# Two pairs' values in one burst at a fused kernel's entry, and an order corrected by a table

## The chip, the cores and the metric

The kernel runs on one core of a Trainium2 chip. Its five engines run side by side and each works through its own instructions in a fixed order: PE (TensorE, matrix products; its weight loads are shown as PEld), DVE (VectorE), ACT (ScalarE), POOL (GpSimd) and SP, which here only issues transfers. The metric is the device time of one execution in microseconds; smaller is better.

## What is computed

Block-causal attention (4 batches, 8 heads, 576 tokens, 64 channels) and two feed-forward layers behind it, all in float32:

```
scores = scale * q @ k.T ; masked where block(i) < block(j), blocks of 64 tokens
attn = exp(scores - rowmax) ; attn = attn / (rowsum + 1e-9)
x = attn @ v                              -> 2304 tokens x 512
x = max(x @ w1, x @ w2, x @ w3) @ w_out   -> 768 wide inside
out = relu(x @ w_in)**2 @ w_out2          -> 2048 wide inside
```

## The kernel before, in words

**Pairs and groups.** Two heads of one batch make a pair; there are 16 pairs, four per batch. The 576 query rows of a pair are cut into two groups: group 0 (rows 0 to 255, steps 0 and 1) and group 1 (rows 256 to 575, steps 2 and 3 and a last half step). A step multiplies scores (tile `sc`), takes the row maximum on DVE (`nm`), the exponential and its row sum on ACT (`P`, `sm`), transposes `P` on PE (`tp`) and copies the result to SBUF: `ta` for group 0, `tb` and `t4` for group 1. Then `values` multiplies the transposed probabilities with v (tile `av`).

**Direct pairs.** For the four pairs of batch 0 the probabilities are not normalised. `sum_rows` spreads the reciprocal row sums over the channels with small products (tile `r`), and DVE multiplies `av` with them. The products `av` and `r` use weights of 64 columns ("narrow"), the two heads side by side; all others load 128 columns ("wide"). A run of narrow products between wide ones is called a burst here.

**The entry.** All four pairs do group 0 first, then group 1. In the same time the weights of the first layer (18 chunks `w1`, 6 chunks `wo1`) are loaded as raw 64-bit words, and each is turned into a high and a low float by two ACT instructions, two DVE instructions, one POOL addition, an ACT copy (high part) and a DVE subtraction (low part). The token block 0 (256 tokens, group 0 of batch 0) goes through the first layer (`l`, from `xhl`, the split of x) between the steps of group 1. The other blocks and batches follow, then the second layer, a stream of products with 384 columns (`ph`, `acc`).

**What sets the order.** The code only records operations. `Plan.issue` then places them: it keeps a modelled clock per engine, and at each step gives the engine that is free first the ready operation of the lowest rank, ties broken by the order of recording. Every instruction is therefore recorded at one helper line of the profile. The plan is made while the program is built; on the chip each engine follows its list and waits where data is missing. The first call of `issue` covers everything up to token block 3; a second call covers the rest.

Of the kernel before, what the change touches and what calls it, by code (L numbers as in the profile page):

```python
# [12 lines left out]
F32 = mybir.dt.float32  # L13
# [10 lines left out]
B, H, S, D = 4, 8, 576, 64  # L24
NPAIR = H // 2
# [12 lines left out]
TAIL = 512  # L38

GROUPS = ((0, 256), (256, 320))  # L40
GA, GB = 256, 320
# [106 lines left out]
        return View(t, t.area)  # L148


class Op:
    def __init__(self, index, engines, name, args, kw, rank):
        self.index, self.engines, self.name, self.args, self.kw, self.rank = index, engines, name, args, kw, rank
        self.deps, self.after, self.makes = set(), [], []
        self.engine = self.end = None

# [15 lines left out]
class Plan:  # L172
# [53 lines left out]
            (v.tile.writes if any(v is x for x in out) else v.tile.reads).append((op, v.area))  # L226
        return op

    def issue(self):

        ops, free, held, queue = self.ops, self.free, self.held, self.queue
        left = [0 for op in ops]
        users = [[] for _ in ops]
        for op in ops:
            for d in (*op.deps, *op.after):
                if d.end is None:
                    left[op.index] += 1
                    users[d.index].append(op)
        waiting = {e: {} for e in free}
        narrow = False  # L240

        def offer(op):
            for e in op.engines:
                when = 0.0
                for d in op.deps:
                    when = max(when, d.end + ((SEM[d.engine] + (500 if e == 'pe' else 100 if e == 'pool' else 0)) if d.engine != e else 0))
                waiting[e][op.index] = when, shares_port(e, op)

        for op in ops:
            if not left[op.index]:  # L250
                offer(op)
        for _ in ops:
            best = None
            for e, w in waiting.items():
                if not w:
                    continue
                other = held["pool" if e == "dve" else "dve"] if e in held else 0.0
                start = {i: max(free[e], at, other if port else 0.0) for i, (at, port) in w.items()}
                t = min(start.values())
                i = min((i for i, s in start.items() if s <= t), key=lambda i: (ops[i].rank, i))  # L260
                if best is None or t < best[0]:
                    best = t, e, i
            t, e, i = best
            op = ops[i]
            op.engine = e
            length = duration(e, op) * SLOW[e]
            if e == "pe":
                length += SWITCH * (columns(op) != narrow)
                narrow = columns(op)
            if e in held and waiting[e][i][1]:  # L270
                held[e] = t + length - HOLD[e]
            for other in op.engines:
                del waiting[other][i]
            if e == "sp":
                queue = max(t + 1700, queue) + transfer(op)
                op.end, free[e] = queue + 300, t + 465
            else:
                op.end = t + length
                free[e] = op.end - LAP[e]
            for tile in op.makes:  # L280
                tile.make()
            self.tc.keep_in_program_order(self.call(self.real[e], alias(e, op.name), op.args, op.kw))
            for u in users[i]:
                left[u.index] -= 1
                if not left[u.index]:
                    offer(u)
        self.ops, self.queue = [], queue
# [74 lines left out]
def fused_kernel(ctx: ExitStack, tc: tile.TileContext, z0, k0, kz0, qk, v, w123, wo1, win2, wo2, out):  # L362
# [164 lines left out]

    ops, x_t = {}, {}
    turn, late = [0], []
    marks = []  # L530

    def new_xf(n):
# [19 lines left out]
    def attn_pair(n, groups=(0, 1)):  # L552
# [5 lines left out]
        direct = n < NPAIR  # L558


        if 0 in groups:
            ta = at.tile([128, 2, GA + 128], F32, tag="ta", bufs=CFG["TB"][0], name=f"ta{n}")
        if 1 in groups:
            tb = [at.tile([128, 4, GB], F32, tag="tb", bufs=2 * CFG["TB"][1], name=f"tb{n}_{h}") for h in range(2)]
            t4 = at.tile([128, 2, 64], F32, tag="t4", bufs=2, name=f"t4_{n}")
        xf = None if direct else new_xf(n)

# [7 lines left out]
        def reciprocals(sm):  # L575
            nc.vector.tensor_scalar(out=sm, in0=sm, scalar1=1e-9, scalar2=None, op0=ALU.add)
            nc.vector.reciprocal(out=sm, in_=sm)


        def step(i):  # L580
            N = 128 * (i + 1)
            name = f"{n}_{i}"

            share = i < 2
            sc = [bank(f"sc{name}_{h}", sc_tag(i)) for h in range(1 if share else 2)]
            P = [at.tile([128, 576], F32, tag="P", bufs=PB, name=f"P{name}_{h}") for h in range(len(sc))]
            if share:
                both = sc[0][:, :2 * N].rearrange("p (h k) -> p h k", h=2)
                sc = [both[:, h] for h in range(2)]
                P = [P[0][:, N * h:N * h + N] for h in range(2)]  # L590
            nm = small(f"nm{name}")
            scale = SCALE if sf else 1.0
            sm = sums[i // 2][:, 2 * (i % 2):2 * (i % 2) + 2] if direct else small(f"sm{name}")
            for h in range(2):
                for c, (qp, kp) in enumerate(score[h]):
                    mm(sc[h][:, :N], qp[:, 128 * i - q0:128 * i - q0 + 128], kp[:, :N], start=c == 0,
                       stop=c == len(score[h]) - 1)
                if not share:
                    nc.vector.memset(sc[h][0:64, N - 64:N], MASKED / scale)
                    nc.vector.tensor_reduce(out=nm[:, h:h + 1], in_=sc[h][:, :N], axis=AX.X, op=ALU.max, negate=True)  # L600
            if share:
                nc.vector.memset(both[0:64, :, N - 64:N], MASKED / scale)
                nc.vector.tensor_reduce(out=nm, in_=both, axis=AX.X, op=ALU.max, negate=True)
            if sf:
                nc.vector.tensor_scalar(out=nm, in0=nm, scalar1=SCALE, scalar2=None, op0=ALU.mult)
            for h in range(2):
                act = nc.scalar.activation(out=P[h][:, :N], in_=sc[h][:, :N], func=AF.Exp, bias=nm[:, h:h + 1],
                                           scale=scale, accum_out=sm[:, h:h + 1])
            if not direct:
                reciprocals(sm)  # L610
                for h in range(2):
                    nc.vector.tensor_scalar(out=P[h][:, :N], in0=P[h][:, :N], scalar1=sm[:, h:h + 1], scalar2=None,
                                            op0=ALU.mult)
            marks.append((act,))
            to = 128 * i - (0 if share else GA)
            tp = [bank(f"tp{name}_{h}", "tp") for h in range(1 if share else 2)]
            for h in range(2):
                t, o = (tp[0], N * h) if share else (tp[h], 0)
                for j in range(i + 1):
                    nc.tensor.transpose(t[:, o + 128 * j:o + 128 * j + 128], P[h][:, 128 * j:128 * j + 128], ident)  # L620
                if not share:
                    cp(CFG["EV2"][h], out=tb[h][:, :i + 1, to:to + 128], in_=t[:, :N].rearrange("p (j q) -> p j q", q=128))
            if share:
                cp(CFG["EV"][i], out=ta[:, :, to:to + N], in_=tp[0][:, :2 * N].rearrange("p (h k) -> p h k", h=2))


        def last_step():
# [17 lines left out]
            marks.append((act,))  # L645
            tp, tq = bank(f"tp{n}_t", "tp"), bank(f"tq{n}_t", "tp")
            for j in range(4):
                nc.tensor.transpose(tp[:, 128 * j:128 * j + 128], P[:, 128 * j:128 * j + 128], ident)
            nc.tensor.transpose(tq[:, :128], P[:, S - 128:], ident)
            for h in range(2):  # L650
                cp("a", out=tb[h][:, :, TAIL - GA:], in_=tp.rearrange("p (j h q) -> p h j q", h=2, j=4)[:, h])
            cp("a", out=t4, in_=tq[:, :128].rearrange("p (h q) -> p h q", h=2))


        def values(g):
            a, w = GROUPS[g]
            acc = bank(f"av{n}_{g}", "av" if g or direct else "tp")
            if g == 0:
                mv = [(0, 0, [ta[:, h, :GA] for h in range(2)]), (1, 128, [ta[:, h, GA:] for h in range(2)])]
            else:  # L660
                mv = [(j, 0, [t[:, j] for t in tb]) for j in range(3)]
                mv += [(3, 128, [t[:, 3, 128:] for t in tb]), (4, 256, [t4[:, h] for h in range(2)])]
            for c, (j, o, p) in enumerate(mv):
                for h in range(2):
                    mm(acc[64 * h:64 * h + 64, o:w], vals[h][j], p[h], start=c == 0, stop=c == len(mv) - 1)
# [12 lines left out]

        def sum_rows(g):
            sm = sums[g]  # L680
            reciprocals(sm[:, :4 + g])
            rows = bank(f"r{n}_{g}", "tp")
            for i in range(2 + g):
                for h in range(2):
                    c, o, m = (2 * i + h, 0, 128) if i < 2 else (4, 64 * h, 64)
# [4 lines left out]
        if 0 in groups:  # L690
# [1 line left out]
                step(i)  # L692
                yield
            if direct:
                values(0)
        if 1 in groups:
            for i in range(2, 4):
                step(i)
                yield
            last_step()  # L700
            yield
            if not direct:
                values(0)
            values(1)

    def split_x(b, j):
        with nc.ranked(CFG["PX"]):
# [149 lines left out]
    with nc.behind(marks[CFG["WO"]][0]), nc.ranked(2):  # L857
        for q in range(NQ):
            quad_forms(1, q)
        for q in range(EARLY):  # L860
            quad_forms(0, q)
    nc.issue()
    es_a.close()


# [310 lines left out]
```

## Time and profile before

| | us |
|---|---|
| median of 3 runs (lowest, highest) | 840.61 (840.38, 841.45) |
| the profiled execution | 840.18 |
| its span, first to last instruction | 838.4 |

The table compares like with like only within a line: the span leaves out what lies around the program, 1.78 us in the profiled execution. That execution is 0.43 us faster than the median. In the rows below "busy" of PE counts a product from its start to its modelled end, and products overlap, so that PE's real pace is read from starts, one product to the next.

### The profile page before, as it was taken

The page shows a single profiled execution, that of the slowest core. Times are in us where ns is not written, and L with a number is a line of the kernel's source. Part 1 is how long each engine was busy: PE and PEld are TensorE (multiplying, and loading weights), DVE is VectorE, ACT ScalarE, POOL GpSimd, SP SyncE. Part 2 cuts the span into 40 slices and gives each one's busy share as a digit, 9 for nine tenths or more (in the row PEclk, how much of TensorE's full clock was granted, in tenths as well). Part 3 has the DMA queues.
Part 4 walks back from the last instruction along what each step waited for, and adds up shares of the span by engine and source line. Part 5 has one row for each costly group of instructions (what it writes and reads, how often), then busy time and mean ns, then how long its engine had stood idle before and what let it go on. Part 6 is the DMA issues. An engine that isn't in the chain of part 4 may idle for free.

```text
span 838.4 us, 14621 instructions
## 1 busy us (share of the span) xinstructions
PE 825.8 (99%) x5008; PEld 779.2 (93%) x5008; DVE 625.0 (75%) x1347; ACT 474.4 (57%) x1099; POOL 108.0 (13%) x98
## 2 busy tenths in 40 slices
PE   8999999999999999999999999999999999999998
PEld 6678899988999889999999999999999999999998
DVE  7989789888889988817877557987269855478562
ACT  7999678788778767736554224544124552233441
POOL 2343111221122212202221000000000000000000
PEclk9999999999999999999999999999999999999999
DMA  9755455665566656254796867888988889988882
GB/s 326 263 162 171 124 175 182 203 224 183 167 206 206 199 192 201 77 194 150 264 352 228 312 203 248 286 292 271 306 257 255 257 249 288 293 256 254 246 272 85
DMA packets 92203, 190.24 MB, mean 227 GB/s; under 512 B 9697, under 2 KB 18913, under 8 KB 92129
## 3 DMA queue, kind: packets, MB, share of 16 engines
q1 hardware_dynamic: 92128, 189.31, 69.2%
q8 instruction: 40, 0.66, 0.3%
q14 instruction: 35, 0.28, 0.1%
HBM read 150.47 MB, written 38.80 MB: 226 GB/s over the span
## 4 chain that ended last, share of the span: by engine, by line
PE 90%; DVE 5%; ACT 3%; DMA 1%; POOL 1%; issue 1%; POOLq 0%; ACTq 0%; DVEq 0%
PE l L190 33%; PE ph_x L190 12%; PE acc_x L190 12%; PE ph_z L190 9%; PE acc_z L190 6%; PE av L190 4%; PE sc L190 4%; PE tp L190 3%; PE acc_y L190 3%; PE sc_t L190 2%; DVE nm L190 1%; DMA raw_w<-in_wo 1%; PE tp_t L190 1%; DVE w1l L190 1%; ACT P L190 1%
## 5 line engine op out<-in xcount | busy, mean ns | idle before, releaser
L190 PE MATMUL l<-xhl,w1h 128*128 128x432 f32 (+2 forms) x864 | 230.6, 344 | 0.5 <-DVE xhl L190 0.5
L190 PEld LDWEIGHTS l<-xhl,w1h 128*128 128x128 f32 x864 | 154.0, 188 | 7.5 <-DVE xhl L190 1.2
L190 PE MATMUL l<-xhl,w1l 128*128 128x432 f32 (+2 forms) x432 | 149.7, 347 | 0.6 <-DVE run L190 0.5
L190 PEld LDWEIGHTS l<-xhl,w1l 128*128 128x128 f32 x432 | 81.3, 188 | 5.8 <-DVE run L190 1.4
L190 PE MATMUL ph_x<-t,ws 128*128 128x384 f32 x432 | 80.9, 335 | 0.0
L190 PE MATMUL l<-hh,wo 128*128 128x432 f32 (+2 forms) x288 | 77.5, 344 | 1.2 <-DVE wo L190 1.1
L190 PEld LDWEIGHTS ph_x<-t,ws 128*128 128x128 f32 x432 | 75.6, 188 | 0.0
L190 ACT ACTIVATE P<-sc,nm 128x128 f32<-128x128 f32 (+3 forms) x128 | 67.3, 535 | 11.5 <-DVE nm L190 10.0
L190 DVE TENSOR_TENSOR run<-l,run 128x432 f32<-128x432 f32 (+2 forms) x72 | 39.8, 553 | 32.6 <-PE l L190 29.4
L190 POOL TENSOR_TENSOR f_w<-f_w,raw_w 128x512 int32<-128x512 int32 x30 | 41.5, 1384 | 148.2 <-DVE f_w L190 33.4
L190 DVE TENSOR_REDUCE nm<-sc 128x2 f32<-128x256 f32 (+2 forms) x96 | 55.0, 590 | 0.8
L190 PEld LDWEIGHTS l<-hh,wo 128*128 128x128 f32 x288 | 51.9, 188 | 3.7 <-DVE wo L190 1.3
L190 PE MATMUL acc_x<-g_p,ws 128*128 128x384 f32 x288 | 54.0, 335 | 0.0
L190 PE MATMUL ph_z<-b,ws 128*128 128x384 f32 x288 | 53.9, 335 | 0.0
L190 PE MATMUL tp<-ident,P 128*128 128x128 f32 x320 | 49.9, 275 | 1.1 <-ACT rs L190 0.5
L190 PEld LDWEIGHTS acc_x<-g_p,ws 128*128 128x128 f32 x288 | 50.5, 188 | 0.0
L190 PEld LDWEIGHTS ph_z<-b,ws 128*128 128x128 f32 x288 | 50.4, 188 | 0.0
L190 PE MATMUL l<-hl,wo 128*128 128x432 f32 (+2 forms) x144 | 49.2, 342 | 0.0
L190 PEld LDWEIGHTS tp<-ident,P 128*128 128x128 f32 x320 | 38.8, 141 | 8.9 <-ACT P L190 1.3
L190 PE MATMUL av<-tb,v 128*64 128x320 f32 (+1 forms) x256 | 42.9, 410 | 0.0
L190 ACT COPY tb<-tp 128x384 f32<-128x384 f32 (+1 forms) x64 | 32.4, 539 | 13.4 <-PE tp L190 12.9
L190 DVE TENSOR_TENSOR g_p<-c_wo,g_p 128x768 fp32r<-128x768 f32 x24 | 22.9, 956 | 16.8 <-ACT g_p L190 16.8
(188 smaller groups left out, 1746.5 us busy)
## 6 DMA issues: line engine op xcount, KB each, us to landing
ws<-ws_d SPq DMA_DIRECT2D x336, 256.0 KB, 4.0
ws_d<-wst SPq DMA_DIRECT2D x70, 256.0 KB, 4.4
raw<-in_qk SPq DMA_DIRECT2D x24, 576.0 KB, 4.3
ws_d<-wst SPq DMA_DIRECT2D x21, 512.0 KB, 7.1
raw_w<-in_w SPq DMA_DIRECT2D x18, 512.0 KB, 4.8
raw_w<-in_wo SPq DMA_DIRECT2D x16, 512.0 KB, 4.3
raw_wi<-in_win SPq DMA_DIRECT2D x14, 512.0 KB, 5.8
v<-in_v SPq DMA_DIRECT2D x16, 320.0 KB, 3.8
```

Source lines behind the costliest of these rows:

```text
L190: return getattr(engine, op_name)(*map(value, args), **{k: value(x) for k, x in kw.items()})
```

## The change

**One burst for two pairs.** In batch 0 an even pair's `values` is kept back and called together with the odd pair's, behind the last copy of the odd pair's transposed probabilities (`done`). So `av` and `r` of two pairs stand in one burst, for either group. For this the odd pair's probabilities go into `home`, a tile in the place of a later x buffer (`xf`), which is empty at that time; `region` finds a chunk's place in it, and the transposes of four chunks are written in a rotated order so that the chunks fit there. The two pairs' `av` of group 0 share one PSUM bank, half each; the odd pair's `av` of group 1 takes a bank of the tag `tp`, its row sums one of the tag `sc`.

**The table.** `issue` gets a list `MOVES` of 424 entries (index of an operation, addition to its rank, addition to its place among equals). It changes the order of the first `issue` all through, on all engines.

```
+MOVES = (
+    (8, -17, -1159), (14, -28, -1568), (16, -16.5, 1598), (17, -11.5, 85), (18, -8.5, 1150), (19, -28.5, -2404),
...
+    def issue(self, moves=()):
...
+        for i, rank, place in moves:
+            ops[i].place = ops[i].rank + rank, ops[i].index + place
...
+                i = min((i for i, s in start.items() if s <= t), key=lambda i: ops[i].place)
...
+    def second():
+        if "home" not in held:
+            held["home"] = m1.tile([128, NPAIR, S], F32, tag="xf", bufs=2, name="home").rearrange("p k s -> p (k s)")
+        return held["home"]
...
+        odd = direct and n % 2
         if 0 in groups:
-            ta = at.tile([128, 2, GA + 128], F32, tag="ta", bufs=CFG["TB"][0], name=f"ta{n}")
+            if odd:
+                ta = second()[:, :2 * (GA + 128)].rearrange("p (h k) -> p h k", h=2)
+            else:
+                ta = at.tile([128, 2, GA + 128], F32, tag="ta", bufs=CFG["TB"][0], name=f"ta{n}")
...
+        def both_values(g):
+
+            reciprocals(sums[g][:, :4 + g])
+            if not odd:
+                held[g] = values
+                return
+            with nc.behind(done[0]):
+                held.pop(g)(g)
+                values(g)
...
+            if direct and g == 0:
+                if not odd:
+                    held["acc"] = bank(f"av{n}_{g}", "av")
+                acc = held["acc"][:, GA * (n % 2):GA * (n % 2) + GA]
+            else:
+                acc = bank(f"av{n}_{g}", "av" if g and not odd else "tp")
...
-            reciprocals(sm[:, :4 + g])
-            rows = bank(f"r{n}_{g}", "tp")
+            rows = bank(f"r{n}_{g}", "sc" if odd and g else "tp")
...
             if direct:
-                values(0)
+                both_values(0)
...
-            if not direct:
+            if direct:
+                both_values(1)
+            else:
                 values(0)
-            values(1)
+                values(1)
...
-    nc.issue()
+    nc.issue(MOVES)
```

The order on PE in the entry. The first number behind a tile's letters is the pair, so `av1_0` is group 0 of pair 1. Before, the burst of pair 1 stands alone between wide products:

```order
L190 MATMUL sc3_0_0_251<-zk_early_107 128x128
L190 MATMUL sc3_1_0_258<-zk_early_107 128x256
L190 MATMUL sc0_2_0_275<-k0_143,z0_qs_139 128x384
L190 MATMUL av1_0_280<-ta1_240,v1_0_103 64x256 x2
L190 MATMUL av1_0_280<-ta1_240,v1_0_103 64x128 x2
L190 MATMUL r1_0_292<-ident_60,sm1_0_203 64x128 x4
L190 MATMUL tp2_0_0_304<-ident_60,P2_0_0_272 128x128 x2
```

Now pairs 0 and 1 stand in one burst (pair 1 writes the other half of the tile `av0_0`):

```order
L269 MATMUL sc3_0_0_240<-zk_early_105 128x128
L269 MATMUL av0_0_243<-ta0_180,v0_0_80 64x256 x2
L269 MATMUL av0_0_243<-ta0_180,v0_0_80 64x128 x2
L269 MATMUL r0_0_255<-ident_60,sm0_0_153 64x128 x4
L269 MATMUL av0_0_243<-home_228,v1_0_110 64x256 x2
L269 MATMUL av0_0_243<-home_228,v1_0_110 64x128 x2
L269 MATMUL r1_0_274<-ident_60,sm1_0_208 64x128 x4
L269 MATMUL sc3_0_0_240<-zk_early_105 128x128
```

The narrow work of two pairs has become one run, later in pair 0's case and with one way in and one way out.

At the end of batch 0, PE's rows around the row sums of pair 3 before, a burst of their own inside the second product of the first layer (`l2`):

```order
L190 MATMUL sc4_2_0_1305<-kh_4_0_1270,qs_4_0_1225 128x384
L190 MATMUL l2_0_1_1255<-hl0_743,wo1_1057 128x256
L190 MATMUL r3_1_1308<-ident_60,sm3_1_1064 64x128 x4
L190 MATMUL r3_1_1308<-ident_60,sm3_1_1064 64x64 x2
L190 MATMUL l2_0_1_1255<-hh0_680,wo1_1057 128x256
```

Now, behind the products of `l2` on the weight chunks 0 to 3, the burst of pairs 2 and 3 begins (32 narrow products, of which these are the first):

```order
L269 MATMUL l2_0_1_1212<-hl0_753,wo1_1045 128x256
L269 MATMUL l2_0_1_1212<-hh0_739,wo1_1045 128x256
L269 MATMUL r3_1_1249<-ident_60,sm3_1_1087 64x128 x3
L269 MATMUL r3_1_1249<-ident_60,sm3_1_1087 64x64
L269 MATMUL av2_1_1254<-tb2_0_865,v2_1_749 64x320
L269 MATMUL av2_1_1254<-tb2_1_935,v2_1_749 64x320
L269 MATMUL r2_1_1259<-ident_60,sm2_1_835 64x128 x3
L269 MATMUL r2_1_1259<-ident_60,sm2_1_835 64x64 x2
L269 MATMUL av3_1_1270<-home_228,v3_1_789 64x320 x3
```

Three runs (pair 2's burst, `av3_1`, `r3_1`), which lay apart before, have become one, and it stands between the uses of chunk 3 and chunks 4 and 5 of `wo1`.

On DVE the low part of chunk 3 of `wo1` (the subtraction `wo1<-f_wo1_3`) stood behind the split of the next x block (`xhl1`) before:

```order
L190 TENSOR_TENSOR run0_5_2_1233<-l1_0_5_2_1206,run0_5_1_1208 128x256
L190 CAST xhl1_1238<-xf0_647 128x320
L190 CAST hh0_680<-run0_5_2_1233 128x256
L190 TENSOR_TENSOR xhl1_1238<-xf0_647,xhl1_1238 128x320
L190 TENSOR_TENSOR hl0_743<-run0_5_2_1233,hh0_680 128x256
L190 TENSOR_TENSOR xhl1_1238<-xf0_647,xhl1_1238 128x320 x2
L190 TENSOR_TENSOR wo1_1057<-f_wo1_3_1124,wo1_1057 128x512
```

Now it stands before it:

```order
L269 TENSOR_TENSOR run0_5_1_1177<-l1_0_5_1_1124,run0_5_0_1100 128x256
L269 TENSOR_SCALAR f_wo1_4_1154<-f_wo1_4_1154 128x512
L269 TENSOR_TENSOR run0_5_2_1182<-l1_0_5_2_1148,run0_5_1_1177 128x256
L269 TENSOR_TENSOR wo1_1045<-f_wo1_3_1112,wo1_1045 128x512
L269 TENSOR_SCALAR nm3_t_1126<-nm3_t_1126 128x1
L269 TENSOR_TENSOR hl0_753<-run0_5_2_1182,hh0_739 128x256
```

The subtraction has moved ahead of the x splits: 192 DVE instructions stand ahead of it instead of 202.

## Rows read from the trace of the kernel before

**Rows 1.** The page's busy times: busy us (share of the span), instructions.

```profile
PE 825.8 (99%) x5008; PEld 779.2 (93%) x5008; DVE 625.0 (75%) x1347; ACT 474.4 (57%) x1099; POOL 108.0 (13%) x98
```

**Rows 2.** Busy us by stretch: stretch, length, PE, PEld, DVE, ACT, POOL; clock; DMA.

```profile
10.00:32.00 22.00, 19.54 (x137) 12.61 (x136) 21.86 (x64) 20.45 (x62) 7.60 (x6) 1.00 0.90 315
32.00:85.00 53.00, 51.91 (x388) 42.12 (x387) 47.83 (x119) 50.37 (x124) 22.04 (x16) 1.00 0.57 182
97.00:360.00 263.00, 261.64 (x1700) 240.05 (x1700) 228.41 (x652) 201.31 (x563) 54.51 (x54) 1.00 0.57 183
440.00:838.40 398.40, 394.80 (x2245) 392.67 (x2243) 261.22 (x382) 147.38 (x241) 2.82 (x2) 1.00 0.80 256
```

**Rows 3.** Timeline of PE, one whole burst: start us, us, product, records.

```profile
40.69 0.28 PE L190 MATMUL l<-xhl,w1l 128*128 128x256 f32 x1
40.81 0.40 PE L190 MATMUL l<-xhl,w1h 128*128 128x256 f32 x2
41.14 2.16 PE L190 MATMUL av<-tb,v 128*64 128x320 f32 x16
...
43.24 0.72 PE L190 MATMUL r<-ident,sm 128*64 128x128 f32 x12
43.90 0.38 PE L190 MATMUL l<-xhl,w1l 128*128 128x256 f32 x1
44.12 0.40 PE L190 MATMUL l<-xhl,w1h 128*128 128x256 f32 x2
```

**Rows 4.** Timeline of PE: pair 3's two bursts and the wait behind them.

```profile
89.13 2.16 PE L190 MATMUL av<-tb,v 128*64 128x320 f32 x16
...
91.34 0.39 PE L190 MATMUL l<-hh,wo 128*128 128x256 f32 x1
91.56 0.28 PE L190 MATMUL l<-hl,wo 128*128 128x256 f32 x1
...
92.90 0.77 PE L190 MATMUL r<-ident,sm 128*64 128x128 f32 x12
93.60 0.38 PE L190 MATMUL l<-hh,wo 128*128 128x256 f32 x1
93.82 0.56 PE L190 MATMUL sc<-kl,qs 128*128 128x128 f32 x3
...
96.24 0.39 PE L190 MATMUL l<-hh,wo 128*128 128x256 f32 x1 [1.13 <-DVE wo L190]
```

**Rows 5.** Timeline of DVE: low parts of wo1's chunks 3 and 4, and 5.

```profile
89.32 1.29 DVE L190 TENSOR_TENSOR wo<-f_wo,wo 128x512 fp32r<-128x512 f32 x2
...
95.49 0.69 DVE L190 TENSOR_TENSOR wo<-f_wo,wo 128x512 fp32r<-128x512 f32 x1 [0.17 <-ACT wo L190]
```

**Rows 6.** Waits of DVE from 10 to 97: us in total, times, longest us.

```profile
DVE sc L190 <- PE sc L190: 2.5, 4, 1.2
DVE nm_t L190 <- PE sc_t L190: 1.5, 2, 0.8
DVE sm L190 <- ACT P_t L190: 0.9, 1, 0.9
```

**Rows 7.** Waits of PE over the span, same columns.

```profile
PE sc L190 <- DMA zk<-in_k: 1.4, 1, 1.4
...
PE tp_t L190 <- DVE P_t L190: 0.6, 1, 0.6
...
PE tp L190 <- ACT rs L190: 0.5, 1, 0.5
...
PE sc_t L190 <- ACT P L190: 0.5, 1, 0.5
...
PE sc L190 <- ACT P L190: 0.2, 1, 0.2
```

**Rows 8.** Instructions by tile, `w1l`: ns min/median/max, first and last start.

```profile
L190 DVE TENSOR_TENSOR w1l<-f_w,w1h x12: 669/684/1720, 17.6 to 71.1; 128x512 fp32r<-128x512 f32 x12
```

**Rows 9.** Timeline of POOL and DVE around the longest of these.

```profile
22.09 1.30 POOL L190 TENSOR_TENSOR f_w<-f_w,raw_w 128x512 int32<-128x512 int32 x1 [1.82 <-ACT raw_w L190]
22.21 1.72 DVE L190 TENSOR_TENSOR w1l<-f_w,w1h 128x512 fp32r<-128x512 f32 x1
```

More of the change, by code (lines that the diff above doesn't have):

```diff
@@ L148, in tile @@
         return View(t, t.area)
+MOVES = (
[74 rows of a table added]
+)
 class Op:
@@ L153, in __init__ @@
         self.index, self.engines, self.name, self.args, self.kw, self.rank = index, engines, name, args, kw, rank
+        self.place = rank, index
         self.deps, self.after, self.makes = set(), [], []
@@ L227, in note @@
         return op
-    def issue(self):
+    def issue(self, moves=()):
         ops, free, held, queue = self.ops, self.free, self.held, self.queue
+        for i, rank, place in moves:
+            ops[i].place = ops[i].rank + rank, ops[i].index + place
         left = [0 for op in ops]
@@ L259, in issue @@
                 t = min(start.values())
-                i = min((i for i, s in start.items() if s <= t), key=lambda i: (ops[i].rank, i))
+                i = min((i for i, s in start.items() if s <= t), key=lambda i: ops[i].place)
                 if best is None or t < best[0]:
@@ L529, in fused_kernel, with region @@
     turn, late = [0], []
+    held = {}
+    def second():
+        if "home" not in held:
+            held["home"] = m1.tile([128, NPAIR, S], F32, tag="xf", bufs=2, name="home").rearrange("p k s -> p (k s)")
+        return held["home"]
+    def region(t, base, first, chunks, a, e):
+        start, w = base + GB * first + a, e - a
+        o = min(start, t.area.shape[1] - GB * chunks)
+        return t[:, o:o + GB * chunks].rearrange("p (j q) -> p j q", q=GB)[:, :, start - o:start - o + w]
     marks = []
@@ L558, in attn_pair @@
         direct = n < NPAIR
+        odd = direct and n % 2
         if 0 in groups:
-            ta = at.tile([128, 2, GA + 128], F32, tag="ta", bufs=CFG["TB"][0], name=f"ta{n}")
+            if odd:
+                ta = second()[:, :2 * (GA + 128)].rearrange("p (h k) -> p h k", h=2)
+            else:
+                ta = at.tile([128, 2, GA + 128], F32, tag="ta", bufs=CFG["TB"][0], name=f"ta{n}")
         if 1 in groups:
-            tb = [at.tile([128, 4, GB], F32, tag="tb", bufs=2 * CFG["TB"][1], name=f"tb{n}_{h}") for h in range(2)]
+            if odd:
+                tb = [(second(), (4 * GB - 128) * h - 128) for h in range(2)]
+            else:
+                tb = [(at.tile([128, 4, GB], F32, tag="tb", bufs=2 * CFG["TB"][1],
+                               name=f"tb{n}_{h}").rearrange("p j q -> p (j q)"), 0) for h in range(2)]
             t4 = at.tile([128, 2, 64], F32, tag="t4", bufs=2, name=f"t4_{n}")
@@ L577, in reciprocals @@
             nc.vector.reciprocal(out=sm, in_=sm)
+        done = []
+        def both_values(g):
[6 more added lines that the diff above has]
+                values(g)
         def step(i):
@@ L619, in step @@
                 for j in range(i + 1):
-                    nc.tensor.transpose(t[:, o + 128 * j:o + 128 * j + 128], P[h][:, 128 * j:128 * j + 128], ident)
+                    to_j = o + 128 * ((j + 1) % 4 if i == 3 else j)
+                    nc.tensor.transpose(t[:, to_j:to_j + 128], P[h][:, 128 * j:128 * j + 128], ident)
                 if not share:
-                    cp(CFG["EV2"][h], out=tb[h][:, :i + 1, to:to + 128], in_=t[:, :N].rearrange("p (j q) -> p j q", q=128))
+                    cp(CFG["EV2"][h], out=region(*tb[h], i == 2, i + 1, to, to + 128),
+                       in_=t[:, :N].rearrange("p (j q) -> p j q", q=128))
             if share:
-                cp(CFG["EV"][i], out=ta[:, :, to:to + N], in_=tp[0][:, :2 * N].rearrange("p (h k) -> p h k", h=2))
+                done[:] = [cp(CFG["EV"][i], out=ta[:, :, to:to + N], in_=tp[0][:, :2 * N].rearrange("p (h k) -> p h k", h=2))]
         def last_step():
@@ L647, in last_step @@
             for j in range(4):
-                nc.tensor.transpose(tp[:, 128 * j:128 * j + 128], P[:, 128 * j:128 * j + 128], ident)
+                o = 128 * ((j + 1) % 4)
+                nc.tensor.transpose(tp[:, o:o + 128], P[:, 128 * j:128 * j + 128], ident)
             nc.tensor.transpose(tq[:, :128], P[:, S - 128:], ident)
             for h in range(2):
-                cp("a", out=tb[h][:, :, TAIL - GA:], in_=tp.rearrange("p (j h q) -> p h j q", h=2, j=4)[:, h])
-            cp("a", out=t4, in_=tq[:, :128].rearrange("p (h q) -> p h q", h=2))
+                cp("a", out=region(*tb[h], 0, 4, TAIL - GA, GB), in_=tp.rearrange("p (j h q) -> p h j q", h=2, j=4)[:, h])
+            done[:] = [cp("a", out=t4, in_=tq[:, :128].rearrange("p (h q) -> p h q", h=2))]
         def values(g):
             a, w = GROUPS[g]
-            acc = bank(f"av{n}_{g}", "av" if g or direct else "tp")
+            if direct and g == 0:
[4 more added lines that the diff above has]
+                acc = bank(f"av{n}_{g}", "av" if g and not odd else "tp")
             if g == 0:
@@ L660, in values @@
             else:
-                mv = [(j, 0, [t[:, j] for t in tb]) for j in range(3)]
-                mv += [(3, 128, [t[:, 3, 128:] for t in tb]), (4, 256, [t4[:, h] for h in range(2)])]
+                mv = [(j, 0, [region(*t, j + 1, 1, 0, GB)[:, 0] for t in tb]) for j in range(3)]
+                mv += [(3, 128, [region(*t, 0, 1, 128, GB)[:, 0] for t in tb]), (4, 256, [t4[:, h] for h in range(2)])]
             for c, (j, o, p) in enumerate(mv):
@@ L701, in attn_pair @@
             yield
-            if not direct:
+            if direct:
+                both_values(1)
+            else:
                 values(0)
-            values(1)
+                values(1)
     def split_x(b, j):
```

73 rows, old and new, of the table MOVES are left out of this document.

## The prediction, made before the changed kernel was run

> **What bounds the kernel now.** I read the page first, then the busy times by stretch, then PE's timeline and the waits of PE and DVE, and last the timelines around the places where PE stands still.
>
> On the page PE looks full [rows 1]: 825.8 of 838.4 us. The stretches say where that is true [rows 2]. From 440 us on PE is busy for 394.8 of 398.4 us and nothing else comes near; the change leaves the order there as it is but for a few rows at the seam, so I put that part at no change. From 97 to 360 PE is busy for 261.6 of 263 us, with DVE at 87%. But from 10 to 32 us DVE is busy for 21.86 of 22 us, so that it has no free time at all, and from 32 to 85 us ACT is busy for 50.37 of 53 us and DVE for 47.83. There three engines run side by side, each nearly full. What they race for shows at 96.24 us: PE has waited 1.13 us for DVE's last weight conversion [rows 4]. From that product on PE runs through with few waits. So the kernel's time is the moment at which PE passes this product (the first use of chunk 5 of `wo1`), plus the PE work behind it, plus the later waits. I make the sum in these three terms.
>
> The same stretches also speak against the change: in the entry it lightens PE, while ACT and DVE, whose work stays the same, are as full [rows 2]. The Trainium skill (Perfetto Trace Analysis, Identifying the Most-Contended Engine) calls the engine with the highest occupancy the one to improve, and wants TensorE judged by its weight loads; by these, PE is at 42.12 of 53 us in that stretch and ACT and DVE come first, so PE's savings there would be worth nothing. That is the second rival below, worked out from rows.
>
> **Seven bursts fewer.** The order has 23 bursts of narrow products before and 16 now: in batch 0, six of group 0 become two and five of group 1 become two; the twelve of the later batches stay. The price of one is in the trace twice. A whole burst of a pair's group 1 (20 records of `av`, 12 of `r`) starts at 41.14, and the second wide product behind it starts at 44.12: 2.98 us for 32 narrow records and one wide product [rows 3]. Pair 3 does the same in two bursts: 89.13 to 91.56 and 92.90 to 93.82, 2.43 + 0.92 = 3.35 us for the same 32 records and two wide products [rows 4]. A wide one of 256 columns takes 0.12 us (40.69 to 40.81), so the second burst costs 3.35 - 0.12 - 2.98 = 0.25 us. The way in comes on top: two wide products start at 40.81, which take 0.24 us, and the burst starts after 0.33 us, 0.09 late. That makes 0.34 us a burst, and 7 x 0.34 = **2.4 us** of PE work less. No instruction is added on PE; the products and copies are the same in number.
>
> **Where this can be cashed.** All seven lie ahead of 96.24, where DVE and ACT are full as well. So I need to know when DVE can have the chunks ready. The new order asks for chunk 3 much earlier: on PE, products on chunks 0 to 3 stand in one run, then comes the burst of pairs 2 and 3, then the products on chunks 4 and 5. Between the first use of chunk 3 and that of chunk 5 there stand now 21 wide products (21 x 0.12 = 2.5), five transposes (0.5), four small scores (0.4) and the burst of 64 records (two whole bursts of 2.98 - 0.12 less one way in and out: 5.5), together 8.9 us. Before it was 91.34 to 96.24 less the wait, 4.9 - 1.1 = 3.8 us [rows 4].
>
> On PE's side, the work ahead of chunk 3's use is smaller by what has gone behind it, the bursts of pair 2 and of pair 3's `av` (2.9 + 2.4), nine wide products (1.1) and five transposes (0.5), and by five saved bursts (1.7): 8.6 us. PE would be there at 91.34 - 8.6 = 82.7 us if it waited elsewhere as before. On DVE's side the low part of chunk 3 was done at about 90.0, the first half of the pair that starts at 89.32 [rows 5]. Ten DVE instructions fewer stand ahead of it; at the mean of the stretch, 47.83 / 119 = 0.40 us, that is 4.0 us, and the large ones among them (x splits) make 3.3; I take 3.5. So DVE has it at 86.5 us if it idles as before. It had 53 - 47.83 = 5.2 us of idle time from 32 to 85 us, so its bounds are 81.3 us (no idle time) and 86.5 us. Of DVE's waits in the entry most are for scores of PE (2.5 and 1.5 us), the rest for ACT [rows 6]. A PE that is early and waits for weights has its scores out early, so I take half of the idle time as gone: 86.5 - 2.5 = 84.0 us. PE then passes chunk 3 at 84.0 and chunk 5 at 84.0 + 8.9 = 92.9 us, against 96.24. The work behind it is larger by about 0.4 us (scores moved there). This term: **-2.9 us**, between -0.4 (86.5) and -5.6 (81.3, for which PE too would have to wait 1.4 us less). The 2.4 us of the bursts are inside it.
>
> **Edits at nothing.** The loads of v move by single places, one of them ahead of the first scores, which start 0.4 us later; PE waits 1.4 us behind these for the next pair's keys anyway, whose place in the queue is the same [rows 7]. If that cover were gone, it would cost the 0.4. The row sums' copies of two pairs share one buffer, so the second pair's x comes about 0.8 us later, behind scores of 2 us on PE. The odd pair's `av` and `r` hold banks of transposes and scores until DVE has multiplied; PE waited 0.5 us in such a place before (`tp` for the copy `rs`) [rows 7]. I put that at 0, with a bound of 4 x 0.5 = 2.0 us; it is inside the upper end of the range. The table costs no instruction.
>
> **Later waits.** Behind 97 us PE waits 0.6 us for normalised probabilities, and 0.5 and 0.2 us for banks that ACT holds [rows 7], 1.3 us in all. In the new order the products between a score and its transpose become more in pairs 12 to 15 and about as many elsewhere. I take **-0.4 us**, between +0.6 (as many new ones, half as long again) and -1.3.
>
> **Sum.** -2.9 - 0.4 = -3.3 us: a profiled execution of 840.18 - 3.3 = 836.9 us. The runs' median lies 0.43 us above the profiled execution, so 837.3 us. What a measurement of this kernel can tell from no change is about 0.2%, 1.7 us.
>
> **One thing that no order decides.** The low part `w1l` takes 0.684 us as a rule and 1.72 us once [rows 8], beside a POOL addition that began 0.12 us before it [rows 9]. So DVE's pace depends on how its instructions fall against POOL's, and the new order deals these anew, by 1 us a time in either direction, which the range has to hold as well. The Trainium skill (SBUF — State Buffer, SBUF: two separate sides) describes the pair of ports that these two engines share as an exclusive lock; the two rows agree with it. Neither the sum nor its bounds use it.
>
> **Rivals.** *The conversions keep their pace.* PE saves its bursts and waits that much longer for chunk 3: DVE at 86.5 us, chunk 5 at 95.4, -0.4 in this term and about the same later: 839.8 us, no change. For it: DVE's 0.14 us of idle time in 22. Against it: 5.2 us of idle time behind that. *All waits go.* DVE loses its whole idle time (-5.6) and the later waits go too (-1.3): 833.7 us. Against it: ACT has 2.6 us of idle time from 32 to 85 us, not 5.2. *Slower: the long burst stands behind a late chunk.* PE's list has 8.9 us of work between chunk 3 and chunk 5 where it had 3.8. If chunk 3's low part comes when it came before, at 90.0 us, PE stands from 82.7 to 90.1, passes chunk 5 at 99.0 and has 0.4 us more behind it: +3.2 us, 843.8 us. It decides against the change from 88.6 us on. For it: its low part is one of 192 instructions on a full engine; against it: it has ten fewer ahead.
>
> **How the numbers follow.** The forecast has 0.52 (its own range 835.6 to 838.8), no change by unchanged pace 0.22, all waits gone 0.13, slower 0.13. Faster by over 0.2%: 0.49 of the forecast and 0.13, 0.62; within 0.2%: 0.25; slower: 0.13. For 8 in 10 I leave out about half of each outer case: 833.9 to 841.0 us.
>
> **What would show it.** PE's starts should show 16 bursts, each way in and out as before; if a joint burst of 64 records takes over 5.8 us, the 0.34 is wrong. PE should wait about a microsecond for chunk 3 near 84 us and pass chunk 5 near 93; DVE's idle time from 32 to 85 us should be about 2.7 us. If PE stands for 3 us or more at chunk 3, the first rival holds; past 88.6 us, the last one. Should DVE's idle time stay near 5 us, I am wrong about what an early PE does for it. New waits of PE for banks behind the joint bursts would show the cost that I put at nothing.

## The result and the profile after

The changed kernel takes 848.68 us (median of 5, 847.97 to 849.43) against 840.38 us of the kernel before (838.57 to 841.45, 5 runs beside it): ratio 1.0104, 95% interval 1.009 to 1.0119. It is slower by 1.0%, 8.3 us. The forecast was 837.3 us, with 0.62 on faster.

The profiled execution has a span of 846.2 us (838.4 before). The page's busy times, as in [rows 1]:

```profile
PE 834.0 (99%) x5008; PEld 782.5 (92%) x5008; DVE 627.2 (74%) x1351; ACT 472.2 (56%) x1095; POOL 109.6 (13%) x98
```

PE has as many instructions as before and is busy for 8.2 us more, and it stands for 12.2 us in all where it stood for 12.6. So it is not waiting that has grown; PE's own work has become longer. The stretches, as in [rows 2]:

```profile
32.00:85.00 53.00, 51.43 (x370) 42.12 (x369) 49.43 (x118) 49.01 (x120) 21.56 (x16) 1.00 0.55 177
97.00:360.00 263.00, 262.84 (x1668) 236.06 (x1668) 225.09 (x641) 193.17 (x540) 53.03 (x53) 1.00 0.56 181
440.00:846.20 406.20, 402.60 (x2285) 400.17 (x2283) 266.43 (x394) 150.69 (x247) 2.59 (x2) 1.00 0.80 257
```

From 97 to 360 us PE now has only 0.16 us without work (1.36 before), at full granted clock, and yet it gets through 32 instructions fewer. Which ones take longer shows when the stretches are asked for the tile `av` alone. The same question to the trace before and to that after, 100 to 400 us (PE's busy time is the first number behind the length):

```profile
100.00:400.00 300.00, 36.99 (x336) 29.91 (x336) 0.00 (x0) 9.64 (x24) 1.00 0.56 182
```

```profile
100.00:400.00 300.00, 44.39 (x336) 31.15 (x336) 0.00 (x0) 9.60 (x24) 1.00 0.55 181
```

The same 336 narrow products of pairs 4 to 15 take 7.40 us longer. Pair 4's burst in PE's timeline before, from its first record to the wide product behind it:

```profile
115.49 0.48 PE L190 MATMUL av<-tb,v 128*64 128x320 f32 x1
...
118.50 0.50 PE L190 MATMUL sc<-kh,qs 128*128 128x128 f32 x2
```

That is 3.01 us. One of the bursts after, pair 5's:

```profile
140.85 2.15 PE L269 MATMUL av<-tb,v 128*64 128x320 f32 x8
142.84 0.22 PE L269 MATMUL av<-t,v 128*64 128x64 f32 x1
142.85 0.43 PE L269 MATMUL av<-ta,v 128*64 128x256 f32 x1
...
142.96 0.82 PE L269 MATMUL av<-ta,v 128*64 128x256 f32 x7
143.55 2.10 PE L269 MATMUL av<-tb,v 128*64 128x320 f32 x8
145.49 0.28 PE L269 MATMUL av<-t,v 128*64 128x64 f32 x2
145.70 0.50 PE L269 MATMUL sc<-kh,qs 128*128 128x512 f32 x1
```

Eight records on `tb` start over 1.99 us, then come the records on `ta`, which serve both heads, and then eight more on `tb` over 1.94 us. Whole, the burst takes 4.85 us; pair 4's takes 3.01 after as well, and before each of the 12 bursts of pairs 4 to 15 does. What sets the two kinds apart is the order on PE, which says whose probabilities each product reads (`tb5_0` is head 0 of pair 5, `tb5_1` head 1):

```
L269 MATMUL av4_1_1588<-tb4_0_1501,v4_0_1300 64x320
...
L269 MATMUL av4_1_1588<-tb4_1_1529,v4_0_1300 64x320
L269 MATMUL av4_1_1588<-tb4_0_1501,v4_0_1300 64x320
L269 MATMUL av4_1_1588<-tb4_1_1529,v4_0_1300 64x320
...
L269 MATMUL av5_1_1982<-tb5_0_1819,v5_0_1310 64x320 x3
L269 MATMUL av5_1_1982<-tb5_0_1819,v5_0_1310 64x192
...
L269 MATMUL av5_1_1982<-tb5_1_1925,v5_0_1310 64x320 x3
L269 MATMUL av5_1_1982<-tb5_1_1925,v5_0_1310 64x192
```

In pair 4 the heads take turns, but for two products of one head at the opening; in pair 5 all products of head 0 in group 1 stand in a row, and later all of head 1's. (Each of these products is two records in the trace.) The two heads of a pair use different column halves of the array. In turns, two 320-column records of different halves start within 0.27 us; in a row, each takes 0.27 us by itself. It is the table that orders pair 5 so: its entries for these products are `(1239, -8.5, -1486), (1240, -5, -1573), (1241, -4, -1676), (1242, -6.5, -1882)` and four more (odd numbers are head 0, even ones head 1), each with a shift of its own, so that the places no longer follow the recording. In 8 of the 16 bursts the turns are broken: pairs 5, 7, 9 and 11 (4.85, 4.52, 4.84 and 4.52 us), 13 and 14 (3.45, 3.44), and the joint ones of pairs 2 and 3 in both groups. The joint bursts show both kinds: in group 0 they take 2.33 us (pairs 0 and 1) and 2.81 us (pairs 2 and 3). Pairs 0 and 1 in group 1, with the turns kept:

```profile
52.10 2.16 PE L269 MATMUL av<-tb,v 128*64 128x320 f32 x16
...
54.76 2.11 PE L269 MATMUL av<-home,v 128*64 128x320 f32 x16
...
56.81 0.72 PE L269 MATMUL r<-ident,sm 128*64 128x128 f32 x12
57.47 0.91 PE L269 MATMUL sc<-k,z_qs 128*128 128x384 f32 x2
```

Pairs 2 and 3, with the turns broken:

```profile
89.76 0.71 PE L269 MATMUL r<-ident,sm 128*64 128x128 f32 x7 [0.25 <-DVE sm L269]
...
91.46 3.08 PE L269 MATMUL av<-home,v 128*64 128x320 f32 x15
...
96.81 0.33 PE L269 MATMUL sc<-kh,qs 128*128 128x128 f32 x1
...
97.97 0.40 PE L269 MATMUL l<-hh,wo 128*128 128x256 f32 x2
```

The two bursts have 64 records of the same shapes; they take 5.37 us in the one and 7.05 us in the other. All narrow bursts together, each from its first start to the start of the wide product behind it, take 61.1 us after and 52.6 us before, although there are seven fewer: 8.5 us, about the whole loss.

Neither the clock nor the transfers explain it. Two stretches, pair 5's burst and pair 6's (3.01 us, turns kept), with the granted clock, the DMA share and GB/s in the last three columns:

```profile
140.85:145.70 4.85, 4.85 (x30) 3.06 (x29) 3.02 (x10) 2.47 (x10) 1.29 (x1) 1.00 0.12 44
161.60:165.00 3.40, 3.40 (x32) 2.83 (x32) 1.59 (x4) 1.24 (x4) 1.53 (x2) 1.00 0.86 268
```

The slow one has the lighter transfers.

### The profile page after: what moved, and what is told of

It is laid out like the page before. It is cut to its first block, busy times and chain, and to the rows that moved or that the text cites. A ratio compares the mean times of both kernels' runs of the same rounds, so it can differ in the third digit from the quotient of the medians.

```text
span 846.2 us, 14589 instructions
## 1 busy us (share of the span) xinstructions
PE 834.0 (99%) x5008; PEld 782.5 (92%) x5008; DVE 627.2 (74%) x1351; ACT 472.2 (56%) x1095; POOL 109.6 (13%) x98
## 4 chain that ended last, share of the span: by engine, by line
PE 90%; DVE 4%; DMA 3%; ACT 3%; issue 1%; POOL 0%; SPq 0%; ACTq 0%
PE l L269 32%; PE ph_x L269 12%; PE acc_x L269 12%; PE ph_z L269 9%; PE acc_z L269 6%; PE av L269 6%; PE sc L269 4%; PE tp L269 3%; PE acc_y L269 3%; DMA raw_w<-in_w 2%; PE sc_t L269 2%; DVE nm L269 1%; DMA zk_early<-in_k 1%; PE tp_t L269 1%; DVE f_w L269 1%
## 5 line engine op out<-in xcount | busy, mean ns | idle before, releaser
L269 ACT ACTIVATE P<-sc,nm 128x256 f32<-128x256 f32 (+3 forms) x128 | 67.4, 536 | 10.5 <-DVE nm L269 6.1
L269 PEld LDWEIGHTS l<-hh,wo 128*128 128x128 f32 x288 | 52.1, 188 | 1.9
L269 PEld LDWEIGHTS tp<-ident,P 128*128 128x128 f32 x320 | 38.5, 140 | 11.4 <-ACT P L269 4.8
L269 ACT COPY tb<-tp 128x384 f32<-128x384 f32 (+1 forms) x56 | 28.7, 538 | 17.6 <-PE tp L269 17.4
L269 DVE TENSOR_TENSOR g_p<-c_wo,g_p 128x768 fp32r<-128x768 f32 x24 | 22.9, 956 | 16.9 <-ACT g_p L269 16.9
```

The lines of the kernel that those rows point to most:

```text
L269: return getattr(engine, op_name)(*map(value, args), **{k: value(x) for k, x in kw.items()})
```

## The experiments

Three theories. H (halves): the loss is the lost turns inside the bursts. E (entry): it is new waits in the first 100 us. R (rest): it is the table's moves of other instructions. Each run was timed beside the kernel before on the same chip (839.58 us in the first four, 839.71 in the last four, which ran on another chip). Differences of about 1 us between one of the first four and one of the last four are therefore read from their traces as well.

**E1, the turns restored.** Operations learn their half, and ahead of issuing, each run of narrow products on PE is put back into the order of recording, in which the heads alternate. Nothing else moves on any engine: in the trace DVE, ACT, POOL and SP have the same instructions in the same order as in the changed kernel.

```
                     mm(acc[64 * h:64 * h + 64, o:w], vals[h][j], p[h], start=c == 0, stop=c == len(mv) - 1)
+                    nc.ops[-1].half = h
...
+            while e < len(pe) and pe[e].half is not None:
+                e += 1
+            if e > a:
+                pe[a:e] = reorder(pe[a:e])
...
+def reorder(burst):
...
+    return sorted(burst, key=lambda op: op.index)
```

> The changed kernel with its table and its order on every engine as it is, except that inside each of its 16 narrow bursts the products stand in the order in which they are recorded, so that the two heads of a pair, which fill the two column halves of the array, take turns. Theory H (lost turns): in the changed kernel's trace two narrow products of opposite halves take 269 ns together at 320 columns, two of one half 269 ns each; the table's order puts one head's products in a row in 8 of the 16 bursts, the bursts take 61.1 us in all instead of 49.7, so this kernel takes about 848.7 - 11.4 = 837.3 us (836 to 840, some of it may come back as waits). Theory E (entry): the loss is new waits for DMA and for conversions in the first 100 us; then the order inside bursts is worth nothing, 847 to 849 us. Theory R (rest of the table): the moves of the other instructions cost it; 847 to 849 us too.

Measured: 837.49 us, ratio to the kernel before 0.9974 (0.996 to 0.9989). The order inside the bursts is worth 11.2 us (about 10.9 by the two ratios to the kernel before, since the changed kernel was timed at another time), and theories E and R fall as causes of the loss. Pair 5's burst in its timeline takes 2.85 us (138.29 to 141.14), and the stretch from 100 to 400 us, asked for `av`, has 35.10 us (second fence):

```profile
138.29 0.87 PE L269 MATMUL av<-ta,v 128*64 128x256 f32 x8
138.99 2.11 PE L269 MATMUL av<-tb,v 128*64 128x320 f32 x16
140.93 0.28 PE L269 MATMUL av<-t,v 128*64 128x64 f32 x4
141.14 0.50 PE L269 MATMUL sc<-kh,qs 128*128 128x512 f32 x1
```

```profile
100.00:400.00 300.00, 35.10 (x336) 22.24 (x336) 0.00 (x0) 9.47 (x24) 1.00 0.57 189
```

**E2, the turns broken in the kernel before**, in the 12 bursts of pairs 4 to 15, with the same means:

```
+    return halves[0] + halves[1] if len(burst) == 14 else burst
```

> The kernel before, with the 14 products of each of the 12 bursts of pairs 4 to 15 in the order of all of head 0, then all of head 1; nothing else moves. Theory H: each of these bursts goes from 3.01 us to 2 x 2.69 + 0.17 = 5.55 us, 12 x 2.54 = +30.5 us, 870.9 us (868 to 872). Theories E and R: the same work in the same bursts, 840.4 us (within 1).

Measured: 865.11 us, ratio 1.0301 (1.0277 to 1.0325), +25.5 us. So the order of the turns alone slows the kernel before as well, with no joint burst, no `home` and no table: 12 bursts that are each 2.16 us longer make 25.9. The size was off: a burst takes 5.17 us, not 5.55. Its timeline for pair 4 shows where the rest went:

```profile
116.97 1.40 PE L190 MATMUL av<-tb,v 128*64 128x320 f32 x5
118.06 0.43 PE L190 MATMUL av<-ta,v 128*64 128x256 f32 x1
118.21 0.33 PE L190 MATMUL av<-tb,v 128*64 128x192 f32 x1
118.32 0.38 PE L190 MATMUL av<-ta,v 128*64 128x256 f32 x1
118.38 0.28 PE L190 MATMUL av<-t,v 128*64 128x64 f32 x2
...
118.76 2.10 PE L190 MATMUL av<-tb,v 128*64 128x320 f32 x8
120.70 0.28 PE L190 MATMUL av<-t,v 128*64 128x64 f32 x2
120.91 0.49 PE L190 MATMUL sc<-kh,qs 128*128 128x128 f32 x2
```

The record on `ta` that starts at 118.06 is head 1's first. By the order, three records of head 0 that start later stand before it: one of 192 columns at 118.21 and the two on `t` from 118.38 on. At the seam the second head begins early, beside the first head's tail.

**E3, strict turns in the kernel before.** The bursts of pairs 4 to 15 begin there with two products of one head, of `av` in group 1 and in group 0. `reorder` is E1's.

> The kernel before with the bursts' products in recorded order: there the 12 bursts of pairs 4 to 15 begin with two products of one head (3.01 us each where strict turns give 2.69 + 0.17 = 2.86). Theory H: 12 x 0.15 = 1.8 us less, 838.6 us. Theories E and R: 840.4 us, no change.

Measured: 837.85 us, ratio 0.9973 (0.9961 to 0.9986), -1.7 us; each of the 12 bursts takes 2.85 or 2.86 us instead of 3.01. Even the kernel before lost a little this way.

**E4, the change without its table.**

```
-    nc.issue(MOVES)
+    nc.issue()
```

> The changed kernel without the table: joint bursts, the shared buffer and the new banks alone, the planner's own order; its bursts take turns but for the opening pair of products (51.9 us in all against 61.1). Theory H: 9.2 us less than the changed kernel from the bursts, and the table's other moves are lost, worth 0 to 4 us: 839.5 to 843.5 us. Theory E (the structure of the entry costs): 846 to 849 us. Theory R (the table's other moves cost): 838 to 841 us, which does not tell it from H; the first run does.

Measured: 844.17 us, ratio 1.0055 (1.0035 to 1.0075), just above the band given for theory H. The bursts do take 52.1 us as expected, but the structure has a cost of its own in the entry. PE's waits from 0 to 97 us (us in total, times, longest), of this kernel and then of the changed one:

```profile
PE tp L269 <- ACT P L269: 6.5, 4, 2.5
...
PE sc L269 <- DMA zk<-in_k: 1.0, 1, 1.0
PE tp_t L269 <- ACT P_t L269: 0.8, 1, 0.8
```

```profile
PE sc L269 <- DMA zk<-in_k: 2.8, 2, 1.8
PE tp L269 <- ACT P L269: 1.9, 5, 0.6
...
PE tp_t L269 <- ACT P_t L269: 0.4, 1, 0.4
```

With the narrow work held back for the odd pair, PE stands for 6.5 us at transposes whose probabilities ACT has not made yet (0.5 us before). The table's moves bring that to 1.9 us. The waits are not all of it. Behind the longest (2.51 us, to 50.56 us) PE's granted clock is 0.75 of the full from 50 to 52 us, 0.50 (the lower level, 1.2 GHz) from 52 to 54 and 0.90 from 54 to 56, where E1 has 1.00 throughout; by these shares that is about 1.7 us of work lost, an estimate.

**E5, the turns restored in pairs 4 to 15 alone**, so that the two broken bursts of batch 0 stay broken:

```
+    return sorted(burst, key=lambda op: op.index) if len(burst) == 14 else burst
```

> The changed kernel with the turns mended in the 12 bursts of pairs 4 to 15 alone; the four bursts of batch 0 keep the table's order (17.6 us in all, 15.4 with turns). Those 12 bursts take 43.5 us in the changed kernel's trace and 34.3 in that of the mended one. If the lost turns of the entry count in full, 848.7 - 9.2 = 839.5 us, 2.0 more than the kernel with all bursts mended (837.5); if weight conversions hide them there, 837.5 us.

Measured: 839.01 us, ratio 0.9992 (0.9983 to 1.0001), 1.5 us behind E1, though the two intervals overlap a little. The traces decide: from the first product on chunk 3 to that on chunk 5 PE takes 11.08 us here and 9.34 us in E1, and the joint burst of group 0 takes 2.81 us instead of 2.32. So the 2.2 us of turns lost in the entry are not hidden by the conversions; the rest of the loss is that of the later pairs.

**E6, the price of a burst.** E3's kernel with each of the 12 later bursts cut in two:

```
+            if e - a == 14:
+                pe[a:e + 2] = pe[a:a + 8] + pe[e:e + 2] + pe[a + 8:e]
```

> The kernel before with strict turns (837.85 us), each of the 12 bursts of pairs 4 to 15 cut in two: two wide instructions that stood behind it now stand behind its first 8 products. The price of a burst in the prediction was 0.34 us. By it 12 more bursts give +4.1 us, 841.9 us. If a way in and out costs no more than the 0.15 us by which a joint burst of 64 records (5.37) is shorter than two of 32 (2 x 2.76), 839.7 us.

Measured: 842.81 us, ratio 1.0037 (1.0025 to 1.0049), 5.0 us above E3, 0.41 us a burst. The traces are closer to the prediction's 0.34: the burst's 28 narrow records and the next eight wide ones take 0.28 to 0.50 us more than in E3 in eleven of the twelve places (median 0.35) and 0.86 us in one.

**E7 and E8, the table in two parts**, on E1's kernel:

```
-    nc.issue(MOVES)
+    nc.issue([m for m in MOVES if m[0] < 1000])
```

E8 is the same with `>= 1000`.

> The kernel with all bursts mended, with those 146 of the table's 424 entries alone that name an operation below 1000 (the entry and the first pairs). The mended kernel takes 739.85 us from its first product on chunk 5 of wo1 to its end, the kernel before with strict turns 739.53: if the rest of the table is worth nothing, 837.5 us (within 1). If it hides waits, as the prediction's last term had it (0.4, up to 1.3 us), 838 to 839 us.

Measured (E7): 838.79 us, ratio 0.9986 (0.9977 to 0.9995), 1.3 us behind E1, with intervals that overlap. The traces do not bear out that the later part of the table is worth anything: from the first product on chunk 5 to the end E7 takes 739.85 us and E1 739.84. The 0.5 us between their spans (835.5 and 835.0) lies ahead of that product, where PE has the same order in both.

> The kernel with all bursts mended, with the other 278 entries alone: joint bursts with the planner's own order in the entry; two of the later bursts come out cut in two (+0.7 us at most). If the structure alone makes the entry late, as the kernel without the table shows it (chunk 5 at 99.0 against 95.15 us, PE waiting for ACT's P up to 2.7 us at a time), 837.5 + 3.9 + 0.7 = 842.1 us. If the table's entries for the entry were worth nothing, 838 us.

Measured (E8): 858.25 us, ratio 1.0223 (1.0209 to 1.0236): a miss by 16 us. The entry is as late as in E4 (first product on chunk 5 at 98.5 us), as expected; what I had not thought of is that the later entries move instructions relative to a plan that now runs otherwise. PE's waits from 97 to 440 us, where the changed kernel has none at all:

```profile
PE tp_t L269 <- DVE P_t L269: 4.0, 2, 3.2
PE l L269 <- ACT run L269: 1.8, 2, 0.9
PE av L269 <- ACT tb L269: 1.0, 2, 0.5
```

The stretch from chunk 5 to the end takes 756.8 us against 739.8 in E1, 17.0 more. The waits from 97 to 440 us make 8.0 of it. Behind the longest (3.2 us) the granted clock is 0.66 of the full from 380 to 390 us, which is 3.4 us of work lost by that share, an estimate. The two bursts that come out cut make 4.7: each part was put into turns by itself, and the parts still hold one head's products in a row (4.93 and 5.48 us instead of 2.85). Two more ways in and out at E6's price make 0.8. Together that is 16.9 us. The table's entries belong to one plan; half of it is not half of its effect, and this run's time says nothing on the price of the entry's part.

## Why the prediction was wrong

**The step that failed** is the one on the bursts, "Seven bursts fewer": "No instruction is added on PE; the products and copies are the same in number", and the sum that only the ways in and out of a burst could change. I priced the narrow products at what they took in the order before and let the table move them freely. Their price depends on who stands next to them. The rows of the new order that stand in the section on the change already end with `av3_1<-home` x3: three products of one head in a row. (The row does not name the head, but in turns six products of 320 columns would stand together. `r3_1` x3 above it is still in turns.) The missing term, by the bursts' own times: 17.6 us in batch 0 where the mended order takes 15.4, and 43.5 us in pairs 4 to 15 where strict turns take 34.3 and the kernel before 36.1. E1 takes the whole of it out and lands at 837.5 us; E2 puts it into the kernel before alone. Between strict turns and the table's order that is 11.4 us. That E1 equals the number forecast is partly luck, as the steps below show.

**The price of a burst** (0.34 us) was right: 0.35 by the median of E6's traces, 0.41 by its time. My test for it, a joint burst of at most 5.8 us, came out at 5.37 and at 7.05 us; the second said that something was wrong, but with the turns, not with the price.

**Chunk 3 and chunk 5.** Forecast: chunk 3 passed at 84.0 and chunk 5 at 92.9 us. DVE's low parts of chunks 3 and 5, as in [rows 5], after:

```profile
86.17 0.68 DVE L269 TENSOR_TENSOR wo<-f_wo,wo 128x512 fp32r<-128x512 f32 x1
...
96.94 0.68 DVE L269 TENSOR_TENSOR wo<-f_wo,wo 128x512 fp32r<-128x512 f32 x1
```

PE passes chunk 3 at 86.99 us and chunk 5 at 98.09 (the second of the two records in the row at 97.97), 1.85 us later than before instead of 3.3 us earlier. Of the 5.2 us between forecast and trace, 3.0 lie ahead of chunk 3 and 2.2 in the stretch behind it, of which the broken turns of the joint burst make 7.05 - 5.37 = 1.7. In E1 the two moments are 85.81 and 95.15 us, 1.1 us earlier than before. So even with turns the term was -1.1 instead of -2.9. DVE's idle time from 32 to 85 us fell from 5.2 to 3.6 us, not to 2.7: in that stretch its waits for `sc` from PE fell from 1.3 to 0.2 us, but those for `sc_t` stayed at 1.5, and one of 0.6 us for ACT's `hh` is new. The low part of chunk 3 comes at 85.7 us in E1, near the bound of a DVE that idles as before (86.5).

The picture of a PE that is early at chunk 3 and stands there was wrong too. PE was to be there at 82.7 us and to wait about a microsecond; it came at 86.99 us (85.81 in E1), and its list of waits has none for `wo`. Part of that is the sum: it moves nine wide products behind chunk 3, where the order moves six (15 stand ahead of it before, 9 now), 0.4 us. Another part is the lost turns of group 0, 0.5 us, which E1 does not have. The rest of PE's lateness is open. At chunk 5, on the other hand, E1 does show the race: DVE waits 1.44 us for ACT's `wo` and has the low part ready at 95.09, and PE's two products there start 0.38 us apart instead of 0.12.

**Edits at nothing.** PE waits 1.9 us for `P` in the entry, 0.4 us before the joint burst for `P_t`, against 0.5 us for `P` before: about 1.8 us more, inside the 2.0 us that I gave as a bound, though not for banks. Its waits for keys (`zk<-in_k`) are 2.8 us against the 1.4 of [rows 7]; E1, with the same order of loads, has 0.8, so that this differs from one execution to the next. E4 shows that the structure without the table costs more, 6.5 us of such waits.

**Later waits.** Forecast -0.4, at best -1.3 us. After the change PE has no wait left behind 97 us; the 1.3 us of [rows 7] that lie there are gone, in the changed kernel in full. E1 has 0.2 us of them and E7, without the table's later entries, 0.9; yet both take the same time from chunk 5 to the end.

**The sum again.** From the first product on chunk 5 to the end: 742.16 us before (838.4 - 96.24), 748.11 after (846.2 - 98.09), +5.95, made of +7.40 for the narrow products and -1.3 for the waits. Ahead of it +1.85. Together +7.8 us of span. Taken without the turns, the change is worth little: E1 (837.49) and E3 (837.85), both with strict turns, are not apart by what these runs can tell.

**The rivals.** None had this mechanism. The slower one came near in its number for the stretch, chunk 5 at 99.0 us, but chunk 3 was in time (its low part done at 86.9, not past 88.6): PE did not stand at chunk 3, it worked longer behind it. With the turns kept, the rival of an unchanged pace of the conversions is the nearest for the entry (it stands first in the list, though the prediction's opening calls it the second): it has chunk 5 at 95.4 us, E1 has 95.15, and the forecast had 92.9.

**The planner** does not see it either. It charges a narrow float32 product by its columns, with an extra only between narrow and wide ones, whatever half stood before it:

```
        if stat.tile.args[1] == F32:
            return n * (0.842 if width(stat) <= 64 else 1.69)
```

0.842 ns a column is the pace of two heads in turns (269 ns for 320 columns, two records of two heads). So a table that is searched by this plan's clock pays nothing for breaking the turns.

## What to carry to other kernels

When a change moves instructions, ask whether an instruction's time depends on its neighbours before taking it as moved at its old price; the narrow products here, which fill a part of the array, do, and the order's rows show it where products of one head stand in a row. Busy time that grows with an unchanged count of instructions points there, and the busy time of one tile, stretch by stretch, shows where. A plan that prices neighbours apart needs a rule that keeps pairs together: restoring the turns behind the plan was worth 11 us here, and 1.7 us in the kernel that nobody had suspected.

## What the runs showed of the hardware

Narrow products of different column halves run side by side (two 320-column records in 269 ns), and those of one half one after another (269 ns each). A shared operand isn't what separates the two cases: in turns the `tb` records overlap, whose heads read different probabilities, and so do the twelve `r` records at 56.81 us in the changed kernel, whose heads read the same `ident` (0.66 us for all twelve). The Trainium skill (TensorE: Matmul & The Clock Gate, Part 3: Packing small matmuls — row/col tiling) says that products on different tiles of the array run concurrently, and the rows agree. It also says that products start strictly in program order. E2's trace differs: a record of head 1 starts at 118.06 us ahead of three records of head 0 that stand before it. Short breaks of the turns cost little (0.15 us a burst in the kernel before) and long ones up to 2.3 us (5.17 against 2.86); that starts can pass each other by a few records fits this, but no run tests it by itself.
